# Retention, MoE and FFN on one core: state products as quarter matmuls, joined tails, and a queue for the weights' scales

## The chip, the cores and the metric

One core of one Trainium2 chip. The time of a run is the device time of one execution in microseconds; a kernel's time is the median of its runs. Besides the runs that are only timed there is one profiled execution, and every row shown here is from that one. PE is TensorE's matmuls (PEld its weight loads), DVE is VectorE, ACT is ScalarE, POOL is GpSimd, SP is SyncE, which issues the DMAs.

## What is computed

```python
# q, k, v: (4, 8, 576, 64) fp32
scores = matmul(q, k.T) / sqrt(64)                 # per sequence and head
Dmat   = gamma[h] ** (i - j) where i >= j, else 0  # decay: retention
x      = matmul(scores * Dmat, v)                  # -> (2304 tokens, 512)
# layer 1: 8 experts, w1[e] (512, 1024), w2[e] (1024, 512)
P      = exp(x @ w_gate - max); 8 times: P /= row sums; P /= column sums; P *= N / E
x      = sum over e of P[:, e] * (relu(x @ w1[e]) @ w2[e])
# layer 2: w_in (512, 2048), w_out (2048, 512)
h      = x @ w_in;  out = max(0.01 * h, h) @ w_out
```

## The kernel before, in words

**Retention** is done in chunks of tokens, with a running state. A chunk is (pb, c, half): the sequence is 2·half + pb, and c counts its 576 tokens as four chunks of 128 and one tail of 64, so there are 20 chunks, 16 full ones and 4 tails. A chunk has all 8 heads, as 4 pairs m of two (j = 0, 1). For a chunk n the program has these steps, and the loop issues them for neighbouring chunks interleaved:

- `emit_qk` (PE, L704): scores k·q of each head into two PSUM banks sc, 8 matmuls that each use 64 of the 128 rows; DVE multiplies them by the decay table into w (L707).
- `emit_state` (PE, L721): the part of the output that comes from earlier chunks: state times decayed q, one 128x128 matmul for each pair, the pair's two 64x64 states standing on the diagonal of a 128x128 block with zeros beside them. None for c = 0.
- `emit_scale` of chunk n-1: l (PE, L764), sums of the absolute outputs over all channels by a matmul with ones, then on DVE a power of two from each sum (s, L772) and the output times it (L774, one instruction on a 128x512 bank).
- `emit_intra` (PE, L731): w times v, added to the state's part in the bank xo; ACT takes absolute values of it (ab, L735).
- `emit_du` (PE, L749): decayed k times v, added up in PSUM (du); ACT copies it to the state (L754), two 64x256 copies.
- `decay_q` (POOL, L680) multiplies q by a table of gamma powers (gq_t), `decay_k` multiplies k by gk_t: heads 0 to 3 on DVE (128x256), 4 and 5 on POOL (128x128, L688), 6 and 7 on ACT (L691).
- `emit_split` (ACT L834, DVE L836) splits the scaled outputs into fp16 high and low parts for the next layer.

The banks sc and xo come from a rotation of five. In each iteration n, PE's order is scores of n+1, state of n, l of n-1, intra of n, du of n. SP issues the loads of q, k, v and of the first weights between these (`load_raw(0, 0)` at n = 2, `load_raw(0, 1)` at n = 6; unit 1's when unit 0's have been split).

**The products.** The rest is 20 units: 16 for the MoE (two for each expert, u = 0 to 15) and four for layer 2 (u = 16 to 19). A unit has two parts of weights (part 0 of w1, part 1 of w2), each 1 MB of fp32 loaded into raw. They are made into fp16 pieces for split products: ACT takes row sums or maxima (L203), a short chain of small instructions on DVE and ACT makes one scale for each part (L209 to L240, with copies L220 and L229 on ACT), ACT multiplies raw by it (L248), ACT casts high pieces (L263, L292) and POOL subtracts and writes the low pieces (L280, L273, L298). For u ≥ 1 the chain is made once for both parts, so it waits for the maxima of both. PE computes hA, hB, hE, hD (L1090, L1059 in unit 0) from the activations' pieces in xring and the weights w, ACT and DVE bend them into hp and hs (L1041 to L1181), PE multiplies these by the second weights into s, s1a, s1b (L1263), and DVE and ACT add them to y (L1273, L1276).

**The turn** (within unit 15 and the start of unit 16) makes layer 2's input out of y: sums of absolute values for each of 9 tile pairs j (L1385, L1387), `norms` on DVE (four small instructions for each j: L162, L163, L1395, L168), POOL scales y (L1402), PE transposes (L1412), and ACT and DVE split the result into xst, from where it goes to DRAM and back into xring.

**The order** of all work that hangs between PE's products is set by `Order`, a planner in the program: tasks stand in queues (evac, turn, gate, hid, weights, late, f64), each with an estimated cost, and each step takes the first ready task within a window of each queue, queue by queue. So an instruction's place on DVE, ACT and POOL follows from these queues; each engine then runs its own list in order.

## Time and profile before

| | us |
|---|---|
| median of 3 runs (lowest, highest) | 1803.91 (1803.06, 1804.24) |
| the profiled execution: time; its span | 1804.81; 1803.0 |
| retention: to the first product of unit 0 | 0 to 85.65 |
| the last step from unit 16's first group into unit 17's first product | about 1517 to 1531 |

The span is 1.8 us shorter than the time of its own execution, and that execution is 0.9 us above the median. The mean granted TensorE clock is 0.992 of full speed. The page says of each engine how much of the span it was busy and follows back the chain of work that ended last; a busy PE is not by that alone a PE at its peak. Where a view has `[2.28 <-ACT w L263]` behind an instruction, the engine stood idle for 2.28 us before it and what came last was ACT's instruction of line 263 that writes w.

### The profile page before, as it was taken

To read this page: it belongs to the slowest core of one execution; us is meant where nothing else is said; L and a number is where in the kernel's file an instruction comes from. 1 tells how busy PE (TensorE), PEld (TensorE's weight loads), DVE (VectorE), ACT (ScalarE), POOL (GpSimd) and SP (SyncE) were. 2 spreads that over 40 slices of the span, in tenths; PEclk is the share of its full clock that TensorE was granted. 3 is DMA by queue.
4 is the path that set the end of the run, shared out by engine and by line. 5 is a ranking of instruction groups with operands and counts; after the bars stand their busy time and mean duration, and the time that the engine had idled before them with its cause. 6 is when DMAs were issued, how large, how long until landed. Compare 5 with 4: busy or idle time off the path is not lost.

```text
span 1803.0 us, 35964 instructions
## 1 busy us (share of the span) xinstructions
PE 1765.5 (98%) x13694; PEld 1288.5 (71%) x13694; DVE 1489.4 (83%) x2657; ACT 1270.9 (70%) x2778; POOL 817.7 (45%) x794
## 2 busy tenths in 40 slices
PE   8999999999999999999999999999999988999998
PEld 7854577777777777777777777777775555777776
DVE  5875898999888888888898888888776895788886
ACT  4856777777777777777777777777675666887653
POOL 2567252626344463626264443635124972443600
PEclk8999999999999999999999999999999999999999
DMA  8953535445354444354453454453442454444232
GB/s 308 319 176 129 159 125 164 137 148 186 116 170 145 149 155 159 126 165 153 132 192 120 158 164 141 143 163 101 132 159 94 157 177 122 130 126 143 79 125 83
DMA packets 206306, 271.82 MB, mean 151 GB/s; under 512 B 13986, under 2 KB 174260, under 8 KB 201012
## 3 DMA queue, kind: packets, MB, share of 16 engines
q1 hardware_dynamic: 206132, 269.52, 46.1%
q8 instruction: 107, 1.75, 0.4%
q14 instruction: 67, 0.55, 0.1%
HBM read 238.66 MB, written 30.81 MB: 149 GB/s over the span
## 4 chain that ended last, share of the span: by engine, by line
PE 84%; DVE 7%; POOL 3%; DMA 3%; issue 2%; ACT 1%; SPq 0%; DVEq 0%; ACTq 0%; POOLq 0%
PE s L1263 17%; PE hA L1090 11%; PE hB L1090 11%; PE hE L1090 11%; PE s1a L1263 11%; PE s1b L1263 11%; PE hD L1090 6%; PE s L1305 1%; DVE xst L566 1%; DVE y L1276 1%; DMA vk<-in_vk 1%; PE s1a L1305 1%; PE s1b L1305 1%; DVE hs L1181 1%; POOL y L1402 1%
## 5 line engine op out<-in xcount | busy, mean ns | idle before, releaser
L1090 PEld LDWEIGHTS <-w 128*128 128x128 f16 x4788 | 468.0, 98 | 247.2 <-issue 3.1
L1263 PEld LDWEIGHTS <-hs 128*128 128x128 f16 x3888 | 380.7, 98 | 88.4 <-DVE hs L1181 4.7
L1263 PEld LDWEIGHTS <-hp 128*128 128x128 f16 x2916 | 285.2, 98 | 82.2 <-issue 3.9
L273 POOL TENSOR_TENSOR w<-raw,w 128x384 f16<-128x384 f32 x148 | 159.1, 1089 | 343.7 <-ACT w L263 343.3
L280 POOL TENSOR_TENSOR raw<-raw 128x256 f32<-128x256 f32 x296 | 272.3, 920 | 19.9
L1276 DVE SCALAR_TENSOR_TENSOR y<-s,fac,y 128x256 f32<-128x256 f32 (+1 forms) x322 | 197.5, 614 | 101.1 <-PE s L1263 83.2
L1263 PE MATMUL s<-w,hs 128*128 128x256 f16 x1932 | 264.9, 274 | 0.8 <-ACT s L1281 0.7
L1090 PE MATMUL hE<-xring,w 128*128 128x384 f16 x1368 | 261.3, 327 | 4.2 <-ACT w L292 2.0
L1090 PE MATMUL hA<-xring,w 128*128 128x384 f16 x1368 | 261.9, 328 | 2.8 <-ACT w L263 2.3
L1090 PE MATMUL hB<-xring,w 128*128 128x384 f16 x1368 | 260.0, 326 | 0.0
L1181 DVE TENSOR_TENSOR hs<-fs,hs 128x768 f16<-128x768 f32 (+1 forms) x228 | 240.0, 1057 | 8.3 <-ACT hs L1171 6.8
L298 POOL TENSOR_TENSOR w<-raw,w 128x512 f16<-128x512 f32 x148 | 200.2, 1368 | 76.1 <-ACT w L292 76.0
L1171 ACT ACTIVATE hs<-fs 128x768 f16<-128x768 f32 (+1 forms) x228 | 187.6, 823 | 46.1 <-DVE fs L1206 36.2
L448 POOL TENSOR_TENSOR f<-f,e 128x256 f32<-128x256 f32 x64 | 51.7, 808 | 363.4 <-DVE e L440 319.4
L1171 ACT ACTIVATE hp<-fp 128x384 f16<-128x384 f32 x240 | 160.3, 677 | 13.9 <-DVE fp L1129 13.2
L1276 DVE SCALAR_TENSOR_TENSOR y<-s1a,fac,y 128x256 f32<-128x256 f32 (+1 forms) x161 | 98.6, 613 | 51.0 <-ACT s L1281 28.7
L1263 PE MATMUL s1a<-w,hs 128*128 128x256 f16 x972 | 133.7, 273 | 4.4 <-ACT hs L1171 2.4
L1276 DVE SCALAR_TENSOR_TENSOR y<-s1b,fac,y 128x256 f32<-128x256 f32 (+1 forms) x161 | 98.7, 613 | 43.8 <-ACT s L1281 18.3
L1263 PE MATMUL s1b<-w,hs 128*128 128x256 f16 x960 | 132.1, 274 | 1.8 <-DVE hs L1181 1.4
L1263 PE MATMUL s1a<-w,hp 128*128 128x256 f16 x972 | 132.6, 273 | 1.1 <-DVE y L1276 1.0
L1263 PE MATMUL s1b<-w,hp 128*128 128x256 f16 x960 | 131.7, 274 | 1.3 <-DVE y L1276 1.3
L1263 PE MATMUL s<-w,hp 128*128 128x256 f16 x966 | 131.8, 273 | 0.0
(213 smaller groups left out, 2766.8 us busy)
## 6 DMA issues: line engine op xcount, KB each, us to landing
xring<-x SPq DMA_DIRECT2D x407, 384.0 KB, 4.0
raw<-in_wm SPq DMA_DIRECT2D x32, 1024.0 KB, 7.7
r<-in_wf SPq DMA_DIRECT2D x64, 256.0 KB, 2.7
x<-xst SPq DMA_DIRECT2D x51, 256.0 KB, 2.3
qk<-in_qk SPq DMA_DIRECT2D x16, 512.0 KB, 4.9
vk<-in_vk SPq DMA_DIRECT2D x16, 512.0 KB, 8.4
wf_s<-f SPq DMA_DIRECT2D x32, 256.0 KB, 3.4
raw<-wf_s SPq DMA_DIRECT2D x8, 1024.0 KB, 6.3
```

The lines of the kernel that those rows point to most:

```text
L273: nc.gpsimd.tensor_tensor(v[0], v[1], v[2], op=ALU.subtract)
L280: nc.gpsimd.tensor_tensor(o, x, y_, op=ALU.subtract)
L298: nc.gpsimd.tensor_tensor(lo, r, hi, op=ALU.subtract)
L448: nc.gpsimd.tensor_tensor(dst, dst, cur["tx"].bitcast(F32), op=ALU.mult)
L566: nc.vector.tensor_tensor(st[d][:, :, 1], src[d](), st[d][:, :, 0], op=ALU.subtract)
L1090: nc.tensor.matmul(bank, w[:, a, wi, k, :], x[:, :, b, k, :], start=r in (1, 5) and k == q == 0, stop=k == 1 and q == 2, skip_group_check= ...
L1171: nc.scalar.activation(hid[k][:, 0, a:b], src[:, a:b], AF.Relu if moe and relu else AF.Copy)
L1181: nc.vector.tensor_tensor(t[:, 1, a:b], src[:, a:b], t[:, 0, a:b], op=ALU.subtract)
L1263: nc.tensor.matmul(out_, t[:, a, i, ts], w[:, b, wi, 0, :], start=start and k == 0, stop=k == 5, skip_group_check=True)
L1276: nc.vector.scalar_tensor_tensor(out_, bank, f, out_, op0=ALU.mult, op1=ALU.add)
L1305: nc.tensor.matmul(bank, t[:, a, i, ts], w[:, b], start=l == g == q == 0, stop=l == g == 1 and q == 2, skip_group_check=True)
L1402: nc.gpsimd.tensor_scalar(y[i], y[i], st["s", j][:, h:h + 1], None, op0=ALU.mult)
```

## The change

In the retention:

- A state is kept as four 64x64 quarters for each j (`[P, NP, D]`) without the zeros, and the state product of a chunk is 8 matmuls, one for each head, that use 64 rows and 64 columns of the array each; the outputs of j = 0 and j = 1 go to two banks x0 and x1 (two buffers each). The scores have a bank each (one buffer), l goes into the free part of x0's bank, du has one bank. So ab and the scaling of the output are two instructions each of half the width, and ACT's copy of the state is one of 128x256 (64 columns for each of 4 pairs) where there were two of 64x256.
- PE's order in an iteration is scores of n+1, state of n, du of n, l of n-1, intra of n.
- `decay_k`: the first two chunks wholly on DVE, else heads 0 to 2 on DVE and 3 to 7 on POOL, none on ACT; ACT loads its table in advance with a one-element instruction.
- The 64-token tails of two sequences make one chunk of 128, so there are 18 chunks: 16 full ones and two joined tails at the end. In these, scores are 16 matmuls of 64x64, two parts of w are set to zero by POOL, and the state product is 16 matmuls of 64 columns.
- `load_raw(0, 0)` at n = 3, `load_raw(0, 1)` at n = 11, both loads of unit 1 after the loop. The host lays out q, k, v in chunks, and w_gate and w1 in the new order of the heads.

Later:

- A queue "scale", ahead of "turn", holds the tasks that make the scales of units 1 and up; and unit 17 (`NU1 + 1`) makes one scale for part 0 from part 0's maxima, and part 1's later.
- In the turn, `norms` is two small instructions for each j, and the inverses are one instruction for three j.

The diff, cut to its core:

```diff
-        self.queues = {q: [] for q in ("evac", "turn", "gate", "hid", "weights", "late", "f64")}
+        self.queues = {q: [] for q in ("evac", "scale", "turn", "gate", "hid", "weights", "late", "f64")}
...
-        sc = scaled(slice(0, 2), maxes(0, ka) + maxes(1, ka), ka)
-        pre0 = scales(0, sc, ka)
+        if u != NU1 + 1:
+            sc = [scaled(slice(0, 2), maxes(0, ka) + maxes(1, ka), ka)] * 2
+        else:
+            sc = [scaled(slice(0, 1), maxes(0, ka), ka)]
+        pre0 = scales(0, sc[0], ka)
         last0 = split(0, 0, pre0[0:2], ka, w1_free(0))
+        if u == NU1 + 1:
+            sc += [scaled(slice(1, 2), maxes(1, k2), k2)]
...
-                for e, h, k in ((nc.vector, 0, 4), (nc.gpsimd, 4, 6)):
...
-                for h in range(6, H):
-                    nc.scalar.activation(kd[:, h], kd[:, h], AF.Copy, scale=gk_t[:, c, h:h + 1])
+                for e, h, k in ((nc.vector, 0, 3 if n > 1 else H), (nc.gpsimd, 3, H if n > 1 else 3)):
...
+        def place(n, m, j):
+
+            i, q = divmod(m, 2)
+            return xo_t[n][j][rows(q), C * i:C * i + C]
...
-                for m in range(NP):
-                    nc.tensor.matmul(xo_t[n][:, place(n, m), :], state[half][:, m, :], qd[:, m * w:(m + 1) * w],
-                                     start=(m == 0), stop=False, skip_group_check=True)
+            for m in range(NP):
+                for b, t in ((pb, slice(0, C)),) if pb is not None else ((0, rows(0)), (1, rows(1))):
+                    for j in range(2):
+                        nc.tensor.matmul(place(n, m, j)[:, t], state[b][half][rows(j), m], qd[rows(j), m, t],
+                                         start=m < 2 and t.start == 0, stop=False, skip_group_check=True)
...
-            nc.vector.scalar_tensor_tensor(xv, xov, XS, sv.unsqueeze(1).to_broadcast([P, NP, w]),
-                                           op0=ALU.mult, op1=ALU.mult)
+            for i in range(2):
+                nc.vector.scalar_tensor_tensor(xv[:, 2 * i:2 * i + 2], xo[i], XS,
+                                               s_t.unsqueeze(1).to_broadcast([P, 2, P]), op0=ALU.mult, op1=ALU.mult)
...
-            if n in (2, 6):
-                load_raw(0, n // 4)
+            if n in (3, 11):
+                load_raw(0, n // 11)
...
-                s2 = st["s", j] = small.tile([P, 2], F32, tag="s2", name=f"ts2{j}")
-                pow2(s1, st["l", j], f"t{j}")
-                nc.vector.tensor_scalar(s2, s1, XS, None, op0=ALU.mult)
-                recip2(inv.rearrange("p (h j) -> p h j", h=2)[:, :, j], s1)
+                s2 = st["s", j] = turn_s[s][:, j - NT_S * s]
+                nc.vector.tensor_scalar(s1.bitcast(I32), st["l", j].bitcast(I32), EXPM, EXPM,
+                                        op0=ALU.bitwise_xor, op1=ALU.bitwise_and)
+                nc.vector.tensor_scalar(s2, s1, XS, XS * 2.0 ** 90, op0=ALU.mult, op1=ALU.min)
```

Two places show what this does to the engines' lists. First PE, within an iteration of the retention loop (n = 6, full chunks): sc are scores, l the sums, w·vk the intra product, and the last row of each piece begins the next iteration. Before:

```order
L704 MATMUL sc_1_590<-qk_452 128x128
L721 MATMUL xo_602<-qd_458,state_139 128x128 x4
...
L764 MATMUL l_147<-ab_563,ones_b 128x128
L731 MATMUL xo_602<-w_535,vk_454 64x128 x8
L749 MATMUL du_145<-vk_454 64x64 x8
L704 MATMUL sc_0_650<-qk_518 64x64
```

The same engine and place (n = 5) with the change:

```order
L695 MATMUL sc_1_531<-qk_377 128x128
L725 MATMUL xo_0_544<-qd_385,state_1_141 64x128
L725 MATMUL xo_1_545<-qd_385,state_1_141 64x128
...
L754 MATMUL du<-vk_379 64x64 x8
...
L764 MATMUL xo_0_468<-ab_504,ones_b 128x128
L735 MATMUL xo_0_544<-w_453,vk_379 64x128 x2
L735 MATMUL xo_1_545<-w_453,vk_379 64x128 x2
...
L695 MATMUL sc_0_593<-qk_444 128x128
```

The state product is eight narrower matmuls that alternate between two banks, du stands behind it, and the sums go into the bank of the chunk before.

Second DVE, where unit 17's first scale is made (pww17, s17, iw17 and sw17 are the small tiles of that chain; y11 and fac16 belong to unit 16's products; xst1_6 and y17 to the turn, the latter being the last tile of unit 15's sums). Before:

```order
L1124 SCALAR_TENSOR_TENSOR fp_100_18313<-hB_1411,p5_100_18265 128x384
L162 TENSOR_SCALAR pww17_0_18383<-m17_17736 128x2
L163 TENSOR_SCALAR s17_17737<-pww17_0_18383 128x2
L168 TENSOR_SCALAR iw17_17735<-s17_17737 128x2
L237 TENSOR_SCALAR sw17_0_18387<-s17_17737 128x1
...
L1276 SCALAR_TENSOR_TENSOR y11_1409<-s2_0_1416,fac16_18034,y11_1409 128x256
```

With the change:

```order
L69 CAST xst1_6_6_17925<-sb1_6_17894 128x2x256
L164 TENSOR_SCALAR pww17_0_17932<-m17_17736 128x1
L165 TENSOR_SCALAR s17_17737<-pww17_0_17932 128x1
L170 TENSOR_SCALAR iw17_17735<-s17_17737 128x1
L239 TENSOR_SCALAR sw17_0_17936<-s17_17737 128x1
L577 TENSOR_TENSOR xst1_6_6_17925<-sb1_6_17894,xst1_6_6_17925 128x2x256
L1270 SCALAR_TENSOR_TENSOR y17_125<-s2_1_1419,fac15_16961,y17_125 128x512
```

The chain, now for part 0 alone, has moved from among unit 16's products up into the turn, before unit 15's last sum is added.

Third ACT, where it casts unit 17's part 0 (w17_0: w0_17_0, from raw17_0) for POOL; hs16 are unit 16's second operands, for tile groups 1_1 and 2_0. Before:

```order
L1273 ACTIVATE y4_115<-s1a_1414,fac16_18034 128x256
L248 ACTIVATE raw17_0_17589<-raw17_0_17589,sw17_0_18387 128x512
L263 CAST w0_17_0_18570<-raw17_0_17589 128x3x128 x2
L292 CAST w0_17_0_18570<-raw17_0_17589 128x4x128 x2
L1041 ACTIVATE fp_101_18487<-fp_101_18487 128x768
```

With the change:

```order
L1275 COPY s2_1_1419<-s1b_1421 128x256
L265 CAST w0_17_0_18183<-raw17_0_17591 128x3x128
L1112 COPY hD_1417<-hB_1415 128x384
...
L1165 ACTIVATE hs16_1_1_18363<-fs_99_18235 128x768
L294 CAST w0_17_0_18183<-raw17_0_17591 128x4x128
L1275 COPY s2_1_1419<-s1b_1421 128x256
L294 CAST w0_17_0_18183<-raw17_0_17591 128x4x128
L1035 ACTIVATE fs_100_18405<-hD_1417 128x384
```

All four casts now stand ahead of the third tile group's operands; before, the last multiplication and all four stood in one block behind y4, a group later.

## Rows read from the trace of the kernel before

**Rows 1.** The page: busy by engine (share, instructions); the chain that ended last, by engine
```profile
PE 1765.5 (98%) x13694; PEld 1288.5 (71%) x13694; DVE 1489.4 (83%) x2657; ACT 1270.9 (70%) x2778; POOL 817.7 (45%) x794
...
PE 84%; DVE 7%; POOL 3%; DMA 3%; issue 2%; ACT 1%; SPq 0%; DVEq 0%; ACTq 0%; POOLq 0%
```

**Rows 2.** Stretches: their us, then busy (instructions) PE, PEld, DVE, ACT, POOL; PEclk, DMA, GB/s
```profile
26.28:85.21 58.93, 57.89 (x931) 53.03 (x927) 52.25 (x120) 49.43 (x128) 29.30 (x34) 1.00 0.88 305
1470.00:1475.00 5.00, 3.73 (x16) 2.46 (x16) 5.00 (x8) 3.16 (x6) 1.31 (x1) 0.50 0.35 141
```

**Rows 3.** Timeline of PE, one full chunk: start, us, line, operation, out<-in, tile, count
```profile
57.61 1.16 PE L704 MATMUL sc<-qk 64*128 64x128 f32 x16
58.70 1.16 PE L721 MATMUL xo<-qd,state 128*128 128x128 f32 x8
59.70 0.39 PE L764 MATMUL l<-ab,ones_b 128*128 128x128 bf16 x4
60.01 1.09 PE L731 MATMUL xo<-w,vk 128*64 128x128 f32 x16
60.94 0.64 PE L749 MATMUL du<-vk 128*64 128x64 f32 x16
61.50 0.72 PE L704 MATMUL sc<-qk 64*128 64x128 f32 x8
```

**Rows 4.** Groups by line and shape, 26.3 to 85.2: busy us, mean ns, idle before
```profile
L707 DVE TENSOR_TENSOR w<-sc,dt_t 128x512 f32<-128x512 f32 x24 | 15.4, 681 | 0.4 <-PE sc L704 0.4
...
L688 POOL TENSOR_TENSOR vk<-vk,gk_t 128x128 f32<-128x128 f32 x13 | 6.6, 506 | 5.0 <-DMA vk<-in_vk 4.7 <-ACT raw L248 0.2
L688 DVE TENSOR_TENSOR vk<-vk,gk_t 128x256 f32<-128x256 f32 x13 | 6.3, 482 | 0.8 <-DMA vk<-in_vk 0.7
L836 DVE TENSOR_TENSOR xf<-y,xf 128x512 f16<-128x512 f32 x6 | 5.6, 928 | 0.0
...
L772 DVE TENSOR_SCALAR s<-l 128x128 int32<-128x128 int32 x14 | 3.9, 281 | 1.2 <-PE l L764 1.2
...
L774 DVE SCALAR_TENSOR_TENSOR tailx<-xo,tails 128x256 f32<-128x256 f32 x2 | 0.8, 425 | 0.2
```

**Rows 5.** Timeline of PE, then of POOL, the first chunks
```profile
16.58 0.70 PE L749 MATMUL du<-vk 128*64 128x64 f32 x8 [3.46 <-POOL vk L688]
17.20 2.08 PE L704 MATMUL sc<-qk 64*128 64x128 f32 x16
...
26.28 1.16 PE L704 MATMUL sc<-qk 64*128 64x128 f32 x16
...
14.90 1.26 POOL L680 TENSOR_TENSOR qd<-qk,gq_t 128x512 f32<-128x512 f32 x1 [14.48 <-DMA gq_t<-in_c_gq]
16.12 0.76 POOL L688 TENSOR_TENSOR vk<-vk,gk_t 128x128 f32<-128x128 f32 x2
```

**Rows 6.** The page: DMA issues, us from issue to landing
```profile
raw<-in_wm SPq DMA_DIRECT2D x32, 1024.0 KB, 7.7
```

**Rows 7.** Timelines of PE, ACT and POOL, the step into unit 17
```profile
1520.08 0.50 PE L1090 MATMUL hA<-xring,w 128*128 128x384 f16 x2 [2.28 <-ACT w L263]
...
1525.80 0.50 PE L1090 MATMUL hE<-xring,w 128*128 128x384 f16 x2 [1.98 <-ACT w L292]
...
1530.94 1.14 PE L1090 MATMUL hB<-xring,w 128*128 128x384 f16 x6
...
1536.49 1.14 PE L1090 MATMUL hE<-xring,w 128*128 128x384 f16 x6
1537.46 0.82 PE L1263 MATMUL s<-w,hs 128*128 128x256 f16 x6
...
1501.63 0.84 ACT L1171 ACTIVATE hs<-fs 128x768 f16<-128x768 f32 x1 [0.52 <-DVE fs L1162]
...
1520.10 1.78 POOL L273 TENSOR_TENSOR w<-raw,w 128x384 f16<-128x384 f32 x2 [37.91 <-ACT w L263]
```

**Rows 8.** Groups of DVE by line, 1420 to 1480
```profile
L162 DVE TENSOR_SCALAR pwt<-tl 128x2 f32<-128x2 f32 x5 | 3.5, 699 | 0.5 <-ACT junk L1385 0.5
```

More of the change, by code (lines that the diff above doesn't have):

```diff
@@ L369, in split @@
             return [add("G", 512, low_t(part, g, h), (ht[h],), key) for h in range(2)]
-        after = lambda part, last, key: add(None, 0, lambda: load_raw(u + 1, part), tuple(last), key, lat=0.5, cond=landed if u else None)
+        after = lambda part, last, key: add(None, 0, lambda: load_raw(u + 1, part), tuple(last), key, lat=0.5, cond=landed if u else lambda: over)
         if u == 0:
@@ new lines, in emit_du, with emit_scale @@
+            nc.scalar.copy(state[pb][half], dus[:, half])
+        def emit_scale(n):
+            j, half = divmod(n, 2)
+            xo, ab = [values(n, i) for i in range(2)], abs_t.pop(n)
+            l1 = xo_t.pop(n)[0][:, 2 * C:2 * C + P]
+            for m in range(NP):
+                nc.tensor.matmul(l1, ones_b, ab[:, m], start=(m == 0), stop=m == NP - 1, skip_group_check=True)
+            xv = halves[n] = half_of(j, half)
+            s_t = last_s if n == N - 1 else awk.tile([P, P], F32, tag="s", name=f"s{n}", bufs=4)
+            nc.vector.tensor_scalar(s_t.bitcast(I32), l1.bitcast(I32), EXPM, EXPM,
@@ L895, in step @@
                         continue
-                    if all(d in popped and wait[0] - popped[d] >= (4 if d.eng == "G" else 2) for d in x.deps):
+                    if (x.cond is None or x.cond()) and all(
+                            d in popped and wait[0] - popped[d] >= (4 if d.eng == "G" else 2) for d in x.deps):
                         pre.remove(x)
@@ L1443, in need @@
     def need(key):
+        order.flush("scale", lambda k: k == key)
         order.flush("weights", lambda k: k == key)
@@ L1502, in retention_moe_ffn_kernel @@
                 w_all[:] = w_all[-120:] + prep_steps(u + 1)
-                order.queues["weights"] += [x for x in w_all if x.key[0] == u + 1]
+                order.queues["weights"] += [x for x in w_all if x.key[0] == u + 1 and x not in order.queues["scale"]]
             if u == NU1 - 1:
```

342 lines of the change are left out of this document (164 added, 178 removed).

## The prediction, made before the changed kernel had run

> **What bounds the kernel now.** I read the page first: PE is busy for 98% of the span and is 84% of the chain that ended last [rows 1]. So time is won only where PE waits, where it does work that can be left out, or where its clock is low. A list of PE's waits by stretch then says where that is: the units in the middle hold nearly none, so three places remain, and I read each by its timeline. They are the retention loop, the turn, and the step into unit 17.
>
> In the loop from the scores of chunk 4 at 26.28 to its end at 85.21, PE is busy 57.89 of 58.93 us at full clock, DVE 52.25, ACT 49.43, the DMA engines 0.88 [rows 2]. So PE bounds it, with DVE 6.7 us behind. A full chunk takes 61.50 - 57.61 = 3.89 us of PE, by the starts: scores 1.09, state 1.00, l 0.31, intra 0.93, du 0.56 [rows 3]. At the step into unit 17 PE waits 2.28 us for ACT's casts of the weights and 1.98 for the next ones; POOL had then been idle for 37.91 us [rows 7], so the weights are late because their scale is, not because an engine was full.
>
> **The state product.** The 16 records of the scores use half the array each and take 1.09 us; the 8 records of the state product use all of it, with as many columns each, and take 1.00 [rows 3]. So two half-array products run beside each other, at 68 ns a record against 125. No row shows quarters. If four run abreast, the new 16 records take half the scores' time, 0.55; if only two, 1.09. A chunk is then 1.09 + 0.55 + 0.56 + 0.31 + 0.93 = 3.44 us, or 3.98. Tile shapes change five times in a chunk instead of three. The six matmuls of hE pass 2304 columns in 0.97 us [rows 7], so the 512 columns of the four for l are worth 0.21; they take 0.31 with a change on either side [rows 3]: at most 0.1 a chunk for two more changes.
>
> The page "TensorEngine Tiling (Array Packing)" of the Trainium skill, section Key Properties, says that tiles operate independently, but that changing the mode drains TensorE. The first sentence would give 0.55, the second speaks against the change; the 0.1 us for two changes agrees that it costs something, 1.4 us for the loop at most.
>
> **The joined tails.** From the scores of chunk 4 on, 17 iterations become 15. Five full ones (n = 3 to 7), two without state (8, 9), five full, one with a tail's shorter scores (about 0.5 less), and two tails, worth some 2.4 and 1.8 us by the same parts (a tail has no du). With 3.44: 10 x 3.44 + 2 x 2.89 + 2.94 + 4.2 = 47.3 us. With 3.98: 39.8 + 5.8 + 3.5 + 4.2 = 53.3. So even in pairs the loop on PE would be 5.6 us shorter than 58.93, by the two iterations that go.
>
> **What DVE makes of it.** Per full chunk DVE now has w 2 x 0.68, s 0.28, two halves of the scaling at 0.425 (the tail's instruction of that shape), 3/4 of the 0.48 for k, and up to n = 13 one split at up to 0.93 [rows 4]: 3.8 us, and 2.85 without split. Over the loop: w 12 x 1.36 + 2 x 1.6, s and scaling 15 x 1.13, k 11 x 0.36, splits 11 x 0.93, some 2 us of small ones: 53 us. That is no less than the 52.25 of before [rows 2], so DVE is the floor as soon as PE is quick. PE alone would end 11.6 us earlier, DVE alone not more than 6. I take 54.5 us, 1.5 us of waits on top of 53: a gain of 4.4, between 1.5 (57.4, in pairs with changes of shape and waits) and 6.4.
>
> The Trainium skill says as much in "TensorEngine Tiling (Array Packing)", section PSUM Bottleneck: tiling speeds up TensorE but not the evacuation of PSUM. By PE alone the sum below would be some 6 us less; the trace agrees with the Trainium skill, since DVE's 52.25 us are there already.
>
> A score bank now has one buffer, so scores of n + 2 wait for w of n + 1. Behind them on PE stands the whole next iteration. w follows the scores at once on DVE, 1.3 us, and is over at about 2.4 of the 3.8 us; s and scaling follow l, at 2.5. That leaves 1.4 us of cover; without it each us of lateness is one on PE. POOL takes five heads instead of two: 2.5 x 0.51 = 1.3 us in place of 0.51 [rows 4], 9 us in all, of which POOL's 29.30 in 58.93 [rows 2] leave room. ACT, at 49.43 us, loses its share of k and gets ab and the state copy in other widths. Neither ends last, so both cost nothing.
>
> **The start.** At 16.58 PE had waited 3.46 us for POOL's k of the first chunks, which stood behind a q that waited for its table until 14.90 [rows 5]. DVE now does both, so du of 0 and 1 no longer wait for that table. What is late next is the table itself: state of 2 at 14.90 + 1.26 = 16.2, then POOL's q of 3 until 17.4 and only then k of 2, 1.3 us, to 18.7, on which du of 2 waits, with l, intra and chunk 4's scores behind it on PE. These take 0.56 + 0.31 + 0.93 = 1.8 us at full clock [rows 3] and twice that at half (scores at 17.20 took 2.08 us [rows 5] against 1.16), so the scores of 4 come at 20.5 to 22.3 instead of 26.28. Gain 4.0 to 5.8; I take 4.5, and 2.5 as the lower end if loads land later. Retention in all: 8.9 us.
>
> **Loads and unit 1.** SP issues raw(0, 0) an iteration later, raw(0, 1) five, unit 1's after the loop. A load takes 7.7 us [rows 6]; unit 0's two groups, some 80 us of PE, hide both of unit 1's. Cost none; were that cover gone, each us late is one us of PE at unit 1.
>
> **The step into unit 17.** From 1517.80, where the wait of 2.28 us begins, to hB at 1530.94 are 13.1 us. The work in it is hA, one s, hE and two halves of s1b: at full clock 0.97 + 0.65 + 0.97 + 1.3 = 3.9, by hE and the start behind it at 1536.49 and 1537.46 [rows 7]. So 9.2 us are lost, in waits and in the low clock that follows them. With the change the scale of part 0 is made in the turn, and the last of its casts on ACT stands right behind the hs of group 1_1, the one at 1501.63 or just after it [rows 7]. So POOL's part, which began at 1520.10 and was over before hB at 1530.94, so 10.8 us at most, can follow from about 1503 and end by 1514. PE wants the weights at 1517.8: 4 us of slack or more. What is late next: ACT, which had idle time in these 13 us, must now do the same casts, bends and sums without; and part 1 and the second group's weights keep their places. I take 8.0 of 9.2, lower end 4.
>
> **The turn.** DVE is full there (5.00 of 5 us) and the clock is at 0.50 in 1470 to 1475 [rows 2]. Two small instructions go for each j, one of them L162's maximum at 0.70 us [rows 8]; the scale's chain of eleven small ones comes in, at no more than that each, so below 8 us against at least 6.3 for the nine j that go, and four multiplications on ACT. Net between a gain of 2 and a loss of 3, taken as 0. Its cover is nil: DVE's list there runs straight into the hs for which PE waits.
>
> **Sum.** 8.9 + 8.0 = 16.9 us off the profiled 1804.81 is 1787.9; the median of before is 0.9 below that execution, so **1787.0**.
>
> **Rivals.**
> - *Pairs and changes of shape.* Quarters run two abreast and the two more changes of shape cost their 0.1 a chunk: 53.3 + 1.4, and 2 us of waits for DVE, 56.7 of 58.93. Then retention gives 2.2 + 4.5 and the time is 1789 to 1790. For it: no row shows four abreast. Against: scores' halves do run together [rows 3]. 0.15. The drain that the Trainium skill names under Key Properties of "TensorEngine Tiling (Array Packing)" would be this rival's second half.
> - *The wait moves.* Unit 17's chain, put into a turn where DVE is full, holds up hs there, or ACT falls behind after 1517: 3 of 8 us remain, 1792. For it: 5.00 of 5 [rows 2]. 0.12.
> - *The step into unit 17 does not change*, because its weights wait for something that I did not see: only retention, 1795. Against: the casts stand a group earlier on ACT. 0.05.
> - *Slower: the clock.* If PE waits for DVE in each chunk, its clock may fall to 1.2 GHz in the loop, as the granted 0.50 in 1470 to 1475, where PE was busy 3.73 of 5 us [rows 2]. Scores then take 2.08 instead of 1.16, a chunk about 6.6, and the loop some 35 us more than 54.5: 1822. It decides from about half of the loop on. Against: with 3.44 of 3.8 us busy PE's gaps are a third of a us. 0.05.
>
> **How the numbers follow.** My forecast has 0.60, the four rivals 0.37, and 0.03 is left for two of them together, which ends within 0.2% of before. 0.2%, 3.6 us, is what a measurement of this kernel can tell from no change. Faster by more: 0.60 + 0.15 + 0.12 + 0.05, less 0.02 for bounds that meet: 0.90; same 0.05; slower 0.05. Low end: start 5.8, loop 6.4, unit 17 9.2, turn 2: 23.4, so 1780. High end, over the third rival: 2.5 + 1.5 + 4 less 3, 1798.
>
> **What would show it.** In the changed trace: state's 16 records in 0.55 or 1.09 us; DVE over 95% busy in the loop; scores of 4 at 20.5 to 22.3; unit 0's first product near 76.7; hA of unit 17 without a wait and the clock at full speed behind it. I am wrong if the period of a chunk stays at 3.9, if DVE's splits grow longer beside a busier POOL, or if the turn's waits grow.

## The result, and the profile after

The changed kernel takes **1786.43 us** (median of 4 runs, 1784.00 to 1786.84), the kernel before 1803.49 in the same session (4 runs, 1799.67 to 1804.24): a ratio of 0.9907, interval 0.9890 to 0.9924. Forecast were 1787.0 and 1780 to 1798. The profiled execution is the one of 1784.00, span 1781.9 against 1803.0.

The page of the changed kernel, PE's line of part 1, the granted clock by slices, and the chain that ended last:

```profile
PE 1750.5 (98%) x13782; PEld 1275.9 (72%) x13782; DVE 1500.0 (84%) x2660; ACT 1262.0 (71%) x2757; POOL 821.7 (46%) x794
...
PEclk9999999999999999999999999999999999999999
...
PE 92%; DVE 3%; POOL 2%; DMA 1%; issue 1%; ACT 1%; SPq 0%; DVEq 0%; POOLq 0%; ACTq 0%
```

PE is still at 98% [rows 1], and it is now 92% of the last chain, not 84%. Of the 21.1 us between the spans, 15.0 are time in which PE was busy (1765.5 to 1750.5) and 6.1 are time in which it stood; a busy PE can also be one at half clock, so this alone does not say what was won. Where the time went is found by reading the start of the same instruction in both traces and following the difference along the program:

| stretch | before | after | difference of the stretch | foretold |
|---|---|---|---|---|
| start: to the scores of chunk 4 | 26.28 | 19.75 | -6.5 | -4.5 |
| loop: from there to unit 0's first product | 59.37 | 57.20 | -2.2 | -4.4 |
| unit 0: to unit 1's first copy of hA on ACT (167.9, 154.6) | 82.2 | 77.7 | -4.6 | nothing |
| units 1 to 14 (to 1400.7, 1385.9) | | | -1.5 | nothing |
| the turn (to 1505.4, 1493.6) | 104.7 | 107.7 | +3.0 | 0 |
| the step into unit 17 and the rest | | | -9.4 | -8.0 |

These make -21.2, the spans' 21.1 to the rounding. The sum that was foretold is 16.9, the medians differ by 17.1. The traces differ by some 4 us more than the medians, since the profiled execution of the changed kernel is its fastest run, 2.4 us below its median, and the one of the kernel before is 1.3 us above its own.

How much a stretch varies between executions is seen in the profiles of the experiments below. Five profiles have the changed kernel's retention (the changed kernel, those without queue, split or both, and the one with the norms as before): the scores of chunk 4 come at 19.66 to 21.59, unit 0's first product at 76.95 to 80.00. The two with the retention of before have their first product at 85.65 and 84.46. Between the means of these the retention gives 7.1 us, and not the 8.7 of the first two lines.

**A chunk.** Timeline of PE in the changed kernel, one full chunk: start, us, engine, line, output and inputs, tile, shape:

```profile
53.61 1.16 PE L695 MATMUL sc<-qk 64*128 64x128 f32 x16
54.70 0.67 PE L725 MATMUL xo<-qd,state 64*64 64x128 f32 x16
55.30 0.69 PE L754 MATMUL du<-vk 128*64 128x64 f32 x16
55.91 0.40 PE L764 MATMUL xo<-ab,ones_b 128*128 128x128 bf16 x4
56.24 1.09 PE L735 MATMUL xo<-w,vk 128*64 128x128 f32 x16
57.26 0.94 PE L695 MATMUL sc<-qk 64*128 64x128 f32 x12
```

By the starts the state product takes 0.60 us, near the 0.55 of four abreast and far from 1.09. The period is 57.26 - 53.61 = 3.65 us instead of 3.89 [rows 3], and no row has a wait. Its parts are 1.09 + 0.60 + 0.61 + 0.33 + 1.02: du (0.56 before), intra (0.93) and l (0.31) each grew a little.

**The loop.** Windows of the changed kernel: the loop from the scores of 4 to its last product, then three parts of it (columns as in [rows 2]):

```profile
19.75:76.08 56.33, 52.89 (x1009) 43.37 (x1007) 53.16 (x133) 36.87 (x98) 32.10 (x33) 1.00 0.91 333
19.75:41.90 22.15, 21.73 (x396) 18.00 (x394) 21.07 (x52) 13.31 (x37) 13.16 (x14) 1.00 0.97 369
...
41.90:65.88 23.98, 22.56 (x394) 18.48 (x393) 23.03 (x53) 17.41 (x44) 14.22 (x13) 1.00 0.87 323
...
65.88:76.08 10.20, 8.59 (x223) 6.88 (x221) 9.06 (x30) 6.15 (x19) 4.72 (x7) 1.00 0.88 277
```

DVE is busy 53.16 us, the foretold 53, but 94% of the loop and not over 95. First PE is the fuller one (21.73 against 21.07), in the middle DVE (23.03 against 22.56), and in the last 10.2 us neither is full. Two groups of DVE's instructions were forecast too short: k and the split for xring. The rows are of the changed kernel, 19.75 to 66, and the last one of the kernel before, 26.3 to 85.2:

```profile
L678 DVE TENSOR_TENSOR vk<-vk,gk_t 128x192 f32<-128x192 f32 x12 | 6.1, 506 | 0.0
...
L831 DVE TENSOR_TENSOR xring<-first,xring 128x512 f16<-128x512 f32 x6 | 5.7, 950 | 0.0
```

```profile
L836 DVE TENSOR_TENSOR xring<-first,xring 128x512 f16<-128x512 f32 x6 | 4.7, 782 | 0.0
```

Three heads of k take 0.51 us where four had taken 0.48 [rows 4], so the price by the head, 0.36, was wrong.

**The step into unit 17.** PE in the changed kernel:

```profile
1505.48 1.14 PE L1084 MATMUL hA<-xring,w 128*128 128x384 f16 x6
1506.46 0.82 PE L1257 MATMUL s<-w,hs 128*128 128x256 f16 x6
1507.12 1.14 PE L1084 MATMUL hE<-xring,w 128*128 128x384 f16 x6
...
1509.40 1.14 PE L1084 MATMUL hB<-xring,w 128*128 128x384 f16 x6
```

From hA to hB are 3.92 us without a wait. By the same rows of before they are 10.86 us, with the wait of 1.98, and 13.14 together with the wait of 2.28 ahead of hA [rows 7]. The full-clock work had been put at 3.9.

### The profile page after: what moved, and what is told of

It reads as the page before. It is cut to its first block, busy times and chain, and to the rows that moved or that the text cites. A ratio compares the mean times of both kernels' runs of the same rounds, so it can differ in the third digit from the quotient of the medians.

```text
span 1781.9 us, 36082 instructions
## 1 busy us (share of the span) xinstructions
PE 1750.5 (98%) x13782; PEld 1275.9 (72%) x13782; DVE 1500.0 (84%) x2660; ACT 1262.0 (71%) x2757; POOL 821.7 (46%) x794
## 4 chain that ended last, share of the span: by engine, by line
PE 92%; DVE 3%; POOL 2%; DMA 1%; issue 1%; ACT 1%; SPq 0%; DVEq 0%; POOLq 0%; ACTq 0%
PE s L1257 17%; PE hA L1084 12%; PE hB L1084 12%; PE hE L1084 12%; PE s1a L1257 12%; PE s1b L1257 11%; PE hD L1084 6%; PE s L1299 2%; PE s1b L1299 1%; PE s1a L1299 1%; PE hE L1053 1%; PE hA L1053 1%; PE hD L1053 1%; PE hB L1053 1%; PE sc L695 1%
## 5 line engine op out<-in xcount | busy, mean ns | idle before, releaser
L275 POOL TENSOR_TENSOR w<-raw,w 128x384 f16<-128x384 f32 x148 | 163.7, 1121 | 311.8 <-ACT w L265 311.2
L300 POOL TENSOR_TENSOR w<-raw,w 128x512 f16<-128x512 f32 x148 | 195.6, 1337 | 96.0 <-ACT w L294 95.9
```

Of the source, the lines that this page charges most:

```text
L275: nc.gpsimd.tensor_tensor(v[0], v[1], v[2], op=ALU.subtract)
L300: nc.gpsimd.tensor_tensor(lo, r, hi, op=ALU.subtract)
```

## The experiments

Each is the changed kernel with one edit (one of them has two), but for one, which is the kernel before with a part of the change. "First product" is the start of unit 0's first product on PE, "unit 0's wait" that of PE for the gate's maximum (mrow) in it, "turn" the stretch of the table above; these three are from the profiled execution. Ratios are to the kernel before on the same chip in the same session (its medians 1803.70, 1803.35, 1802.55). The changed kernel itself ran only beside the 1803.49, so differences from its median carry some 1 us between sessions besides the scatter of the runs.

| kernel | median us | ratio, interval | first product | unit 0's wait | turn |
|---|---|---|---|---|---|
| before | 1803.49 | 1 | 85.65 | none (another, 1.8) | 104.7 |
| changed | 1786.43 | 0.9907, 0.9890 to 0.9924 | 76.95 | none | 107.7 |
| neither queue nor split | 1797.35 | 0.9962, 0.9948 to 0.9976 | 77.00 | 2.7 | 104.7 |
| queue, no split | 1794.67 | 0.9944, 0.9929 to 0.9960 | 78.67 | 2.7 | 105.8 |
| split, no queue | 1794.25 | 0.9950, 0.9937 to 0.9963 | 77.07 | 2.7 | 107.7 |
| before with queue and split | 1796.60 | 0.9959, 0.9944 to 0.9974 | 84.46 | none (another, 1.8) | 107.6 |
| norms as before | 1787.07 | 0.9909, 0.9894 to 0.9923 | 80.00 | none | 107.6 |
| quarters in another order | 1787.14 | 0.9905, 0.9889 to 0.9922 | 76.64 | 2.7 | 107.1 |
| l ahead of du | 1787.44 | 0.9907, 0.9892 to 0.9922 | 75.88 | 2.7 | 107.5 |
| l ahead of du, tables later | 1786.08 | 0.9913, 0.9899 to 0.9926 | 75.07 | 0.6 | 109.3 |
| k on DVE and POOL from the start | 1796.00 | 0.9957, 0.9940 to 0.9973 | 87.09 | 2.7 | 107.7 |
| k all on DVE | 1787.44 | 0.9911, 0.9896 to 0.9926 | 79.05 | none | 109.3 |
| last v and k earlier | 1788.62 | 0.9921, 0.9906 to 0.9935 | 75.32 | 2.7 | 109.2 |
| raw earlier | 1784.96 | 0.9902, 0.9887 to 0.9916 | 77.93 | none | 108.0 |

### Unit 17: the queue and the split

Neither:

```diff
-            if u:
-                order.queues["scale"] += tasks[first:]
...
-        if u != NU1 + 1:
+        if True:
...
-        if u == NU1 + 1:
-            sc += [scaled(slice(1, 2), maxes(1, k2), k2)]
```

> The changed kernel with only unit 17's part taken back: one scale for both parts of its weights, and no queue ahead of the turn's for the scales. Theory (the step into unit 17 waits for its scale, and making it early in the turn costs the turn a little): the wait for ACT's first casts comes back, with the low clock behind it, some 9.4 us; the turn gets back 1.4 us that it lost between the two traces; so about 1794 us, 8 us above the changed kernel. Rival (the wait would be gone anyway, since the retention and the shorter norms moved the work around it): within 3 us of the changed kernel's 1786.4.

1797.35, 10.9 us more than the changed kernel, where 8 had been expected; the turn gets back 3.0 us and not 1.4. PE of this kernel at the step:

```profile
1511.05 0.50 PE L1080 MATMUL hA<-xring,w 128*128 128x384 f16 x2 [1.67 <-ACT w L265]
1512.40 0.66 PE L1080 MATMUL hA<-xring,w 128*128 128x384 f16 x3 [0.85 <-POOL w L275]
...
1517.12 0.50 PE L1080 MATMUL hE<-xring,w 128*128 128x384 f16 x2 [2.86 <-ACT w L294]
1518.36 1.61 PE L1080 MATMUL hE<-xring,w 128*128 128x384 f16 x4 [0.74 <-POOL w L300]
```

The waits of [rows 7] are back, so queue and split took them away. Next the queue alone, which is the changed kernel with only the last two pieces of this diff, and the split alone, with only the first piece:

> The changed kernel with the queue for the scales kept, but one joint scale for both parts of unit 17's weights. In its list on ACT the first cast of part 0 stands ahead of the hs of group 2_0, the other three behind it, one place above where they stand without queue and split. Theory (the scale is late because it waits for the maxima of part 1, which is loaded last; the queue alone can't help): most of the wait at unit 17 remains, 1793 to 1797, near the 1797.4 of the kernel with neither. Rival (the queue does the most): under 1790.

> The changed kernel with unit 17's two separate scales kept, but no queue for them ahead of the turn's: the chain of the first scale stands behind the turn's last work on DVE, the casts for hA by the hs of group 1_1, the last cast for hE only behind the hs of group 2_0, where both stood before the change. Theory (each cast that stands early takes away its own wait): hA doesn't wait, hE waits 2 to 3 us with the low clock behind it, and the turn is 1 us shorter than with the queue; 1789 to 1792. Rival (the split alone is all that is needed): 1785 to 1787.

1794.67, as expected, and 1794.25, some 2 us above what was expected: by medians each alone gives about 3 of the 10.9 us, as much as their intervals leave open. With the queue alone hA still waits 1.18 us for ACT's cast and hE 2.87; with the split alone hA waits for nothing and hE 2.3 us in three waits for POOL. So the split brings the weights for hA in time, and those for hE need both.

The traces part the two better than the medians. From the end of the turn to the end of the kernel they show 297.0 us with neither, 296.5 with the queue alone, 291.5 with the split alone, and 288.3 with both; so both give 8.7 us there, the split alone 5.5, the queue alone 0.5. The turn gets longer by 1.1 us with the queue, 2.9 with the split and 3.0 with both. This makes 5.7 us for both, not 10.9. Another 5.5 us lie in unit 0, which takes 83.2 us in the profile with neither and 77.7 in the changed kernel's; it is treated below.

The other way round, both put into the kernel before:

> The kernel before with only the queue for the scales and unit 17's two separate scales added. Theory (this part stands by itself): 1803.5 - 9.4 + 1.4, about 1795.5 us, with the step into unit 17 free of waits and the turn 1 to 2 us longer. Rival (the gain needs the shorter norms, since the chain is put into a turn where DVE is full): the turn loses 5 us or more and the time stays above 1799.

1796.60, 7.1 less than before, near the expected 8: the part works without the retention's, and 10 us of the 17 are the retention's and unit 0's. hA and hE wait for nothing, and the turn is 2.9 us longer, not 1 to 2. The 7.1 here and the 10.9 above differ by less than their intervals together, so what the part is worth stays between 5.7 and 10.9.

### The turn: the norms

```diff
-                nc.vector.tensor_scalar(s1.bitcast(I32), st["l", j].bitcast(I32), EXPM, EXPM,
-                                        op0=ALU.bitwise_xor, op1=ALU.bitwise_and)
-                nc.vector.tensor_scalar(s2, s1, XS, XS * 2.0 ** 90, op0=ALU.mult, op1=ALU.min)
+                pow2(s1, st["l", j], f"t{j}")
+                nc.vector.tensor_scalar(s2, s1, XS, None, op0=ALU.mult)
+                recip2(inv.rearrange("p (h j) -> p h j", h=2)[:, :, j], s1)
```

> The changed kernel with the four small DVE instructions for each tile pair of the turn instead of two and a joint inverse. Theory (DVE is full in the turn, so 0.85 us more for each of the pairs is late for PE where its waits are): the turn grows by 2 to 4 us, 1788.5 to 1790.5. Rival (PE waits there for POOL's scaling and for a chain over ACT, and DVE's small instructions fit in between): within 1.5 us of 1786.4.

1787.07, below what the theory expected, and its turn takes 107.6 us like that of the changed kernel: the shorter norms gave nothing that a run shows. The table says what cost there: 104.7 us in the kernel before and without queue and split, 105.8 with the queue alone, 107.1 or more in every kernel with the split. Why it is 109.2 or 109.3 in three of them is not shown. Windows over that stretch, first the changed kernel, then the one with neither:

```profile
1385.90:1493.60 107.70, 95.98 (x585) 58.74 (x584) 94.69 (x144) 72.18 (x157) 80.81 (x72) 0.97 0.49 161
```

```profile
1392.70:1497.40 104.70, 95.04 (x586) 58.53 (x585) 89.55 (x145) 71.44 (x157) 71.89 (x64) 0.98 0.50 165
```

PE does the same work, but POOL is busy 8.9 us longer with 8 instructions more, and DVE 5.1 us longer with one instruction less. The split brings unit 17's casts and subtractions into the turn, and DVE's instructions are longer beside the busier POOL: the eight that write hs (128x768) take 1.19 us each in the changed kernel and 1.00 in the other. That this makes the 3.0 us is argued and not shown, since with the split alone the turn is as long (107.7) while POOL is busy 75.55 us in it and DVE 91.08. PE waits longer for hs, first in the changed kernel, then in the one with neither:

```profile
1457.23 0.61 PE L1257 MATMUL s1a<-w,hs 128*128 128x256 f16 x2 [4.13 <-ACT hs L1165]
...
1480.83 1.14 PE L1084 MATMUL hB<-xring,w 128*128 128x384 f16 x6 [1.90 <-ACT hB L1094]
```

```profile
1462.45 0.39 PE L1253 MATMUL s1a<-w,hs 128*128 128x256 f16 x2 [3.04 <-ACT hs L1161]
```

### The loop: what a chunk costs PE

Quarters with the four of one j one after another, and not j = 0 and 1 in turns:

```diff
-            for m in range(NP):
+            for j in range(2):
...
-                    for j in range(2):
+                    for m in (0, 2, 1, 3):
```

> The changed kernel with the 8 state matmuls of a chunk in another order: those of one quarter of the array stand behind each other (j outside, m in the order 0, 2, 1, 3), the work is the same. Theory (four quarters run abreast, but only as the order brings neighbours from different quarters): state's records take 0.9 to 1.6 us instead of 0.60, the period of a chunk grows from 3.65 by as much, over 13 chunks with state 4 to 13 us: 1790 to 1799. Rival (the engine finds quarters that are free whatever the order is, or the 0.60 has another reason): period and time unchanged, 1786.

PE of this kernel:

```profile
47.23 0.69 PE L725 MATMUL xo<-qd,state 64*64 64x128 f32 x16
47.85 0.69 PE L754 MATMUL du<-vk 128*64 128x64 f32 x16
```

The state product took 0.62 us (47.23 to 47.85) instead of 0.60, and the time is 1787.14. The theory that neighbours must lie on different quarters fell: these two orders of the quarters take the same time.

l ahead of du, so that a chunk has four changes of tile shape and not five:

```diff
             emit_state(n)
-            emit_du(n)
             if n >= 1:
                 emit_scale(n - 1)
+            emit_du(n)
```

> The changed kernel with the sums l of chunk n-1 issued before du of chunk n instead of behind it, so that du and the intra product, which use the array in the same shape, stand together: four changes of shape in a chunk instead of five. Theory A (PE bounds the loop, and a change of shape costs about 0.1 us): period 3.65 to 3.55, 1 to 1.5 us less in all, 1785. Theory B (DVE is the floor of the loop): period and time unchanged. Rival C (l now comes before ACT has the absolute values): waits of 0.3 us or more at l in most chunks, 1787 to 1791.

PE of this kernel, a full chunk:

```profile
30.97 1.16 PE L695 MATMUL sc<-qk 64*128 64x128 f32 x16
32.06 0.67 PE L725 MATMUL xo<-qd,state 64*64 64x128 f32 x16
32.66 0.40 PE L764 MATMUL xo<-ab,ones_b 128*128 128x128 bf16 x4
32.99 0.69 PE L754 MATMUL du<-vk 128*64 128x64 f32 x16
33.51 1.04 PE L735 MATMUL xo<-w,vk 128*64 128x128 f32 x16
34.48 0.71 PE L695 MATMUL sc<-qk 64*128 64x128 f32 x8
```

The period is 3.51 us, 0.14 less: du and intra, now of one shape behind each other, take 0.52 and 0.97 instead of 0.61 and 1.02. That DVE lets a shorter period through shows that PE sets it in such chunks. The first product comes 1.07 us earlier than in the changed kernel, and earlier than in all five profiles with that retention. The time does not follow: 1787.44, where the theory had 1785; and unit 0 has its wait of 2.7 us. To take that wait away, the first task of the queue f64 (the pair of L432 and L433 on DVE) was moved later:

```diff
-            a = Task("D", 500, first(n), tuple(last), "f64", lat=0.5 if n else 8.0)
+            a = Task("D", 500, first(n), tuple(last), "f64", lat=0.5 if n else 20.0)
```

> The changed kernel with l issued before du (as in the run with l first), and with the first piece of the work that turns layer 2's 64-bit weights into fp32 held back by some 12 us, so that DVE's reduction of the gate's maximum (mrow) stands ahead of it and no longer behind it. In most runs so far PE waited 2.7 us for that reduction in unit 0, with a lower clock behind it, and not in the profiled execution of the changed kernel, where POOL was idle beside DVE's two instructions ahead of it. Theory (that wait is real in most executions, and l first is worth 1 us): 1782 to 1784, and a narrower spread of the runs. Rival (the wait only moves to the next step of the gate, and l first is worth nothing): 1785.5 to 1788.

The wait shrank to 0.6 us, and unit 1 began as early as in the changed kernel (154.5), but the turn took 109.3 us, and the median is 1786.08, not 1782 to 1784. The runs spread from 1784.67 to 1790.82, wider and not narrower. The expected gain is not there.

All of k on DVE:

```diff
-                for e, h, k in ((nc.vector, 0, 3 if n > 1 else H), (nc.gpsimd, 3, H if n > 1 else 3)):
+                for e, h, k in ((nc.vector, 0, H), (nc.gpsimd, H, H)):
```

> The changed kernel with k of every chunk scaled wholly by DVE, none by POOL: on DVE an instruction of 128x512 (0.95 us by two of the kernel before at 0.48, 1.25 by the one of the first chunks) in place of one of 128x192 (0.51). Theory (DVE, with 53.16 of 56.33 us, stands right behind PE): 12 chunks at 0.44 to 0.74 more make 58 to 62 us on DVE, so the loop is 3 to 6 us longer and the time 1789 to 1793. Rival (DVE's instructions get shorter by as much when POOL is idle, or the slack of DVE is larger than its busy share says): the loop within 1 us, the time 1786 to 1787.5.

Its windows over the loop:

```profile
18.99:78.10 59.11, 53.21 (x1003) 43.60 (x1002) 56.70 (x134) 37.22 (x97) 23.79 (x20) 1.00 0.91 328
```

The loop is 59.11 us instead of 56.33: of 3.5 us more work on DVE 2.8 came through, so DVE stands right behind PE. The bigger instruction cost less than either price put to it, 0.81 us in the mean in place of 0.51, beside a POOL that is busy 23.79 instead of 32.10 us:

```profile
L678 DVE TENSOR_TENSOR vk<-vk,gk_t 128x512 f32<-128x512 f32 x13 | 10.5, 806 | 1.2 <-DMA vk<-in_vk 1.2
```

The price of 1.25 was misread: in the changed kernel's first two chunks this instruction takes 0.68. The loop's 3 to 6 us were just missed, and the time, 1787.44, is in the rival's range, only 1.0 above the changed kernel's; a difference of this size is within what the runs scatter.

### The start

```diff
-                for e, h, k in ((nc.vector, 0, 3 if n > 1 else H), (nc.gpsimd, 3, H if n > 1 else 3)):
+                for e, h, k in ((nc.vector, 0, 3), (nc.gpsimd, 3, H)):
```

> The changed kernel with k of the first two chunks scaled as in all others, heads 0 to 2 on DVE and 3 to 7 on POOL. Theory (the start was won because du of 0 and 1 no longer stand behind a q that waits for its table): POOL does q of 2 from 14.55 to 15.9, k of 0 and 1 by 17.3, q of 3 by 18.6 and k of 2 by 19.3, so the scores of 4 come 1.4 to 2.5 us later than the changed kernel's 19.75, and the time is 1788 to 1789. Rival (the new order of PE and the earlier clock won the start, and POOL's place there doesn't matter): scores of 4 within 0.7 us of 19.75, the time 1786 to 1787.

PE of this kernel, from du of the first chunk to the scores of chunk 4:

```profile
17.25 0.90 PE L754 MATMUL du<-vk 128*64 128x64 f32 x10 [7.84 <-POOL vk L678]
18.08 2.08 PE L695 MATMUL sc<-qk 64*128 64x128 f32 x16
...
20.94 2.67 PE L695 MATMUL sc<-qk 64*128 64x128 f32 x16 [0.78 <-DVE w L697]
...
30.72 1.16 PE L695 MATMUL sc<-qk 64*128 64x128 f32 x16
```

1796.00: the theory's sign, four to seven times its size. Two instructions on DVE instead of POOL are worth 9.6 us. POOL kept the times expected of it to 0.7 us; what the expectation left out is that du of chunk 0 stands ahead of the scores of chunk 1 on PE, so the whole program waits with it, and that PE comes out of the wait at half clock (0.50 in 18 to 26, against 1.00 in the changed kernel). The scores of 4 come at 30.72 and not 19.75.

### The tails and the loads

The last chunk's v and k an iteration earlier:

```diff
             load_vk(n + 2)
+            if n == N - 4:
+                load_vk(N - 1)
```

> The changed kernel with one thing moved: the v and k of the last chunk (17) are issued one iteration earlier, ahead of the loads of xring. In the changed kernel's trace SP issues that load at 69.01, behind loads of xring that stand on SP from 63.9 to 69.0, and intra of chunk 17 then waits 0.65 us for it at 75.05 (1.7 in another kernel's trace). Theory (the order on SP makes the tails late, and PE sets the rest): the wait is gone, unit 0's first product comes 0.6 to 1.2 us earlier, the time is 1785 to 1786. Rival (DVE's output of the chunk before, 0.75 us late at 73.04, takes its place, or xring comes later by as much): unit 0's first product within 0.3 us of 76.95, the time 1786 to 1787.

In the changed kernel the tails hold these waits and then unit 0's first product:

```profile
73.04 1.04 PE L725 MATMUL xo<-qd,state 64*64 64x64 f32 x32 [0.75 <-DVE y L770]
...
75.05 1.09 PE L735 MATMUL xo<-w,vk 128*64 128x128 f32 x16 [0.65 <-DMA vk<-in_vk]
...
76.95 0.65 PE L1053 MATMUL hA<-xring,w 128*128 128x384 f16 x3
```

With that load earlier, the second wait is gone and the first product comes at 75.32, 1.63 us earlier, more than expected. Yet the median is 1788.62 where 1785 to 1786 had been expected: unit 0 has its wait, and the turn takes 109.2 us. The raw weights nearly as before:

```diff
-            if n in (3, 11):
-                load_raw(0, n // 11)
+            if n in (3, 7):
+                load_raw(0, n // 7)
...
-        after = lambda part, last, key: add(None, 0, lambda: load_raw(u + 1, part), tuple(last), key, lat=0.5, cond=landed if u else lambda: over)
+        after = lambda part, last, key: add(None, 0, lambda: load_raw(u + 1, part), tuple(last), key, lat=0.5, cond=landed if u else None)
```

> The changed kernel with the loads of the weights nearly as before: the second part of unit 0's at n = 7 instead of 11, and unit 1's free to go before the loop has ended. Theory (the loads are hidden at either place): the period of a chunk stays within 0.1 of 3.66, unit 0's first product within 0.7 of 76.95, the time 1785.5 to 1787.5. Rival (the loads collide with v and k in the loop, whose DMA engines are 0.91 busy, and were moved for that): PE's waits for v and k grow by 2 us or more in sum and the time is 1788.5 to 1791.

1784.96, the lowest median of all, but its interval (0.9887 to 0.9916) holds the changed kernel's ratio, so it beats nothing for sure. The first product comes at 77.93, within the 76.95 to 80.00 of the profiles with the loads as in the changed kernel: the loads are hidden at either place, as far as these runs can tell.

### Unit 0: where earlier retention is lost again

In seven of the twelve profiles of kernels with the changed retention PE waits 2.7 us in unit 0, always at the same s1a. From its first product to unit 1's first copy of hA, unit 0 then takes 81.5 to 84.3 us; it takes 79.5 in the one where the wait is 0.6, and 77.7 to 78.0 in the four without it (the changed kernel, norms as before, k all on DVE, raw earlier). The two profiles with the retention of before have 82.2 and 81.1, with another wait, of 1.8. DVE, POOL and PE there, first in the changed kernel, where that wait is absent, then in the one with the last v and k earlier:

```profile
144.08 0.29 DVE L432 TENSOR_SCALAR f<-r 128x256 int32<-128x256 int32 x1 [0.19 <-DMA r<-in_wf]
144.28 0.29 DVE L433 TENSOR_SCALAR e<-r 128x256 int32<-128x256 int32 x1
144.49 0.55 DVE L1175 TENSOR_TENSOR hp<-fp,hp 128x384 f16<-128x384 f32 x1
144.96 0.27 DVE L972 TENSOR_REDUCE mrow<-s1a 1x1 f32<-1x128 f32 x1
...
144.59 2.09 POOL L275 TENSOR_TENSOR w<-raw,w 128x384 f16<-128x384 f32 x2 [1.12 <-ACT w L265]
```

```profile
143.85 1.00 DVE L432 TENSOR_SCALAR f<-r 128x256 int32<-128x256 int32 x1
144.78 1.00 DVE L433 TENSOR_SCALAR e<-r 128x256 int32<-128x256 int32 x1
145.69 1.50 DVE L1177 TENSOR_TENSOR hp<-fp,hp 128x384 f16<-128x384 f32 x1
147.12 0.27 DVE L974 TENSOR_REDUCE mrow<-s1a 1x1 f32<-1x128 f32 x1
...
143.47 2.15 POOL L275 TENSOR_TENSOR w<-raw,w 128x384 f16<-128x384 f32 x2
...
147.44 2.44 PE L1301 MATMUL s1a<-w,hp 128*128 128x512 f16 x6 [2.71 <-DVE mrow L974]
```

In the first, POOL stood idle for 1.12 us until 144.59, just while DVE did the pair of L432 and L433: 0.29 us each. In the second POOL worked through, and the same two took 1.00 each and the next 1.50 instead of 0.55, so the maximum came 2.2 us later and PE's next matmuls took 2.44 instead of 1.46. The rest of the changed kernel's trace bears it out: of its 128 instructions of these two lines, the 85 that ran with POOL idle took 0.28 or 0.29 us, and of the 43 that ran at least in part beside POOL 23 took 1.00 to 1.25. In the three other profiles without the wait POOL also stands idle ahead of the same instruction, for 1.02 to 1.56 us.

The Trainium skill, page "SBUF — State Buffer", section "SBUF: two separate sides", says that VectorE and GpSimd share one pair of ports, and that a VectorE instruction in a two-port mode or with two SBUF inputs and a GpSimd instruction exclude each other there, the later one waiting for the whole length of the first. These rows agree in kind; which port an instruction held is in no trace.

Whether the changed kernel's other three runs, 2.0 to 2.8 us above its profiled one, have this wait is not shown: only one execution has a trace, and where the profiles show the wait it costs some 4 us or more.

## Why the prediction was right, and where it was not

- **Time.** 1787.0 against 1786.43, within the range, and on the foretold side. That it is so near is partly luck. In the two traces the stretches with a forecast came to 15.1 us (6.5, 2.2 and 9.4, less 3.0) for the 16.9 foretold; another 6.1 lie in units 0 to 14, for which nothing was foretold; and the medians differ by 4 us less than these traces. The terms that were off cancelled, as follows.
- **State in quarters: right.** Four abreast, 0.60 us. The rival of pairs fell.
- **The period, 3.44: mis-sized.** Measured 3.65. The changes of shape were the short term, "at most 0.1 a chunk for two more": going from five to four gives back 0.14, and the two that came in make up the 0.21 over the foretold 3.44, so each costs 0.1 or a little more. For the loop this is some 3 us and not 1.4. The Trainium skill, "TensorEngine Tiling (Array Packing)", section Key Properties, says that changing the mode drains TensorE; the 0.1 us a change agrees in sign.
- **DVE is the floor: half right.** Its 53 us came out (53.16), but by luck: they were a sum of rows, and the rows of the changed kernel's loop add up to 60.4 (58.9 before, for a busy time of 52.25 [rows 2]), because an instruction of DVE can start before the last one has ended (144.28 in the rows above, behind 144.08 and 0.29). k took 6.4 us for 13 and not 4.0, the splits 11.3 and not 10.2, the small ones 5.8 and not 2; that the overlap was not taken off made up for it. The split for xring grew from 0.78 to 0.95 us, which is in part the foretold sign of being wrong; the split for xf stayed at 0.93. And with a period of 3.65 PE is as late as DVE: l ahead of du shortens the period to 3.51, so PE sets it there, and of each us added to DVE 0.8 come through in the loop.
- **The loop, 4.4: mis-sized.** 2.6 us by the windows. The term that was off is the 1.5 us of waits on top of DVE's 53: the loop is 3.2 us longer than DVE is busy, about a third of it in each of the three parts. Behind it stand the period and the waits of PE, 3.0 us in all. At the tails, 10.2 us with 8.59 of PE, it waits for DVE's output and for a v and k that SP had issued behind xring's loads; queue order on SP was looked at for raw alone. And du of one chunk waits 0.98 us for POOL's k, which had been priced as costing nothing. With the load of the last v and k earlier, 55.7 us go from the scores of 4 to unit 0's first product, against 57.2.
- **The start, 4.5: right in kind, mis-sized.** 6.5; the scores of 4 at 19.75, ahead of the foretold 20.5 to 22.3. In the four other profiles with this retention it is 4.7 to 6.6. Two rows of the changed kernel's POOL and PE:

```profile
17.13 0.72 POOL L678 TENSOR_TENSOR vk<-vk,gk_t 128x320 f32<-128x320 f32 x1
...
17.90 0.56 PE L754 MATMUL du<-vk 128*64 128x64 f32 x10 [0.98 <-POOL vk L678]
```

  Five heads on POOL took 0.72 us (0.82 in the mean of the loop, where two had taken 0.51 [rows 4]), and not the 1.3 of a price by the head; so du of 2 went on at 17.9 and not 18.7. And PE's clock was already full, 1.00 in 10 to 20 against 0.67 before, with its wait of 3.46 us gone.
- **Unit 0's first product: right.** 76.95 for the foretold 76.7, with a start that gave more and a loop that gave less; the profiles with the same retention reach to 80.00.
- **Unit 0: missing.** The kernel before lost time there to a wait of 1.8 us and a clock of 0.89 in 140 to 155; the changed kernel's profiled execution has neither, which is worth 4.6 us. I had read "loads and unit 1: none" and not looked at the gate. By the other kernels it is not the change's gain but a meeting of DVE and POOL that comes out either way: seven profiles with the changed retention take 81.5 us or more there.
- **The step into unit 17: right.** 9.4 against 8.0, hA without a wait and at full clock. The mechanism held: the last casts right behind the turn's hs, POOL's part in its idle time. POOL was earlier than foretold: six of its eight instructions for part 0 ran at 1470.36 to 1477.77, inside the turn, and the last ended at 1493.14, 12.3 us ahead of hA, where 4 us or more had been foretold. By medians 10.9 us hang on queue and split, by the traces of the kernels with and without them 8.7 less the turn's 3.0. 5.5 more lie in unit 0, which has its wait in one of these two profiles and not in the other; whether the medians hold it too is not settled.
- **The turn, 0: mis-sized at its bound.** +3.0, the loss that closed the range. The cause was another than the one priced: not the scale's chain or the norms (1.1 and nothing), but the split, which brings unit 17's weights into the turn. "POOL's part can follow from about 1503" was priced as free because POOL was idle, and neither its earlier start nor its work beside a full DVE was charged. That POOL's work made DVE late is the likely way, and not shown.
- **The slower rival fell:** the clock is 1.00 in the loop, where PE waits 3.0 us in all and never more than 0.98 at a time.

## What to carry to other kernels

Work that is moved into an engine's idle time is free for that engine only: where VectorE is full, ask what GpSimd will do beside it and price VectorE's instructions by rows with GpSimd busy. Microseconds won ahead of a place where several engines meet (a gate, a turn) are sure only as far as that place; follow the difference of the two traces beyond it before counting them. In a start-up, an instruction on which the first matmuls wait can cost more than that wait: here 7.84 us at one du made the scores of chunk 4 come 11 us later, with everything behind it on TensorE waiting and the clock at half. And one trace of each kernel is one draw: with the same retention the first product came anywhere from 76.95 to 80.00, and unit 0 took 77.7 us in one trace and 81.5 in another with nothing changed but the order of the matmuls in the state products ahead of it.

## What the runs showed of the hardware

Sixteen records of 64 rows by 64 columns and 128 moving columns ran four abreast, at 38 or 39 ns a record in both orders tried. A change of tile shape cost about 0.1 us (a period of 3.65 us with five changes, 3.51 with four). GpSimd's product of 128x320 took 0.82 us in the mean of the loop, where one of 128x128 had taken 0.51 [rows 4]. VectorE's 128x256 int32 instruction took 0.28 or 0.29 us with GpSimd idle and up to 1.25 beside it.
